# Batch 7's attention moves out of the plain blocks into the first contraction of the second layer's second pair

## The chip, the core and the metric

One core of a Trainium2 chip runs the whole program. The metric is the device time of one execution in microseconds (us). The engines are named as in the profile: PE (TensorE matmul) with its weight loads PEld, DVE (VectorE), ACT (ScalarE), POOL (GpSimd) and SP (SyncE, which issues most DMAs). Each engine takes its instructions in the order in which the program holds them; SP and ACT also issue DMAs from that order.

## What is computed

```python
kv  = einsum('bhsd,bhse->bhde', k, v)          # 8 batches, 8 heads, s = 576, d = 64
out = einsum('bhsd,bhde->bhse', q, kv)
x   = out / sqrt(mean(out*out, -1) + 1e-6) * g_norm     # -> 4608 tokens x 512
h   = x @ w_in1                                # 512 -> 2048
g   = where(h >= 1, h, where(h <= -1, 0, (h + 1)**2 / 4))
x1  = g @ w_out1                               # 2048 -> 512
r   = maximum(x1 @ w_in2, 0)
out = (r * r) @ w_out2
```

All of it is float32; a product of the two layers is made of three matmuls on values split into a high and a low part (`hi*hi + hi*lo + lo*hi`).

## The kernel before

**Two stretches.** Batches 0 to 4 go through layer 1 as plain blocks of 512 tokens (`h_stage`, `out_stage`, matmuls of line 246). Everything else is done in pairs of token blocks by a seven-product scheme (fewer multiplications, more additions): `PAIRS = [(1, 5), (2, 0), (2, 2), (1, 7), (2, 4), (2, 6)]`, each a layer and its first block, and a short rest step at the end. Steps are counted n = 0 to 6; n = 2 is layer 2's second pair.

**A step of a pair** has a first contraction (`in_phase(n)`, 512 to 2048) and a second one (`out_phase(n)`, 2048 to 512), 336 matmuls each, all of line 927. The first goes through four quarters q = 0 to 3; a quarter has seven products p in the order `PRODUCTS = (1, 6, 2, 7, 5, 4, 3)`, and each product has two halves k = 2q and 2q + 1 of six matmuls. Products 1 and 2 of a half add up in one PSUM bank (named `ph2_1_k`), 6, 7 and 4 in a second (`ph2_6_k`), 5 and 3 in a third (`ph2_5_k`); so `ph2_5_3<-x2_2_3_0` is product 3 of half 3. In between the bank is read: DVE adds (`e16`, `e167` at line 977, `h` at line 984), ACT applies the ReLU and the square in place (lines 991, 992). At the end of a quarter DVE makes sums of the results (`t1`, `g2`, lines 1000 and 1001). The second contraction takes operands t that ACT rounds to the high part (line 225) and DVE completes with the low part (line 856), three ahead (`LEAD = 3`); its first eight (`t2_1_0` to `t2_1_7`) stand in a ring of five slots, three of pool `gp` and two of `wp`.

**Attention** of one batch is four head pairs hp. `kv_stage` makes k-transposed times v of two head pairs in one PSUM bank (`pkv`), ACT copies it to `kvbd`; `t_stage` transposes q on DVE (`qT`, line 564); `o_stage` makes each half of the output (`po`, line 591), which ACT reads three times (squares `s2` and `wk0`, scaled `wk1`; lines 596, 597, 217) and DVE once (`s2lo`, line 602); `r_stage` sums squares on PE (`pr`, line 616), then ACT takes Ln, Exp and a square (lines 617, 619, 232) and DVE a Newton step and the scaling (lines 530, 533, 534). `po`, `pr` and `pkv` share the two banks of pool `ps_t` (tag `at`). The tiles `wk0`, `wk1`, `wk2`, `hl0` and `hl1` have one buffer each; `wk2` holds `s2` first and then `t`.

**Where attention stands.** In the plain stretch hooks put it between the plain blocks, at numbered half steps: `STARTS` gives the first of each head pair of batches 2 to 7. Batch 7 has no plain block; its results `xt`, `xr` go to DRAM (`keep_x`, lines 640 and 641) and are read back as input of step 3 (`x2_jobs`). Its four head pairs are spread over batches 4 to 6 and one behind them.

**What sets the order.** The tile layer records the program and then a list scheduler writes each engine's order by its own estimate of readiness, so an instruction can stand far from its place in the source. A tile waits for the last user of its buffer.

Of the kernel before, what the change touches and what calls it, by code (L numbers as in the profile page):

```python
# [76 lines left out]
def linear_attention_rms_two_mlps(  # L77
# [12 lines left out]
    nc = tc.nc  # L90
# [18 lines left out]
    STARTS = (32, 39, 46, 53, 60, 66, 72, 78, 84, 90, 96, 102, 109, 115, 121, 127, 133, 139)  # L109
    STARTS += (145, 151, 156, 161, 166, 173)  # L110
# [30 lines left out]
    PAIRS = [(1, PLAIN), (2, 0), (2, 2), (1, B - 1), (2, 4), (2, 6)]  # L141
    LAST_B = B - 1
# [461 lines left out]
    def r_stage(b, hp):  # L604
# [63 lines left out]
    def attention(starts, order):  # L668

        slots = []  # L670
        for j, (s, (b, hp)) in enumerate(zip(starts, order)):
            turn.setdefault((b, hp), len(turn))
            if b == 1:
                slots += [(max(0, s - 7), load_kv, b, hp), (s, kv_stage, (b, hp))]
            elif j % 2 == 0:
                two = order[j : j + 2]
                turn[two[1]] = len(turn)
                slots += [(max(0, s - 7), load_kv, *i) for i in two]
                slots.append((s, kv_stage, *two))
            slots += [  # L680
                (max(0, s - 7), load_q, b, hp),
                (s, t_stage, b, hp),
                (s + 3, o_stage, b, hp, 0),
                (s + 4, o_stage, b, hp, 1),
            ]
            if hp == 0 and b < LAST_B:
                slots.append((s + 6, begin, b))
            slots.append((s + 6, r_stage, b, hp))
            if b == LAST_B:
                slots.append((s + 8, keep_x, b, hp))  # L690
            elif hp == NP - 1:
                slots.append((max(2 * NF * b, 0) if b < PLAIN + 1 else s + 9, store_xrem, b))
        return slots
# [129 lines left out]
    t1_ring = Ring(*[(st, "st")] * 7, (dt, "dt3"))  # L823
    v_ring = Ring(*((wp, f"w0_{i}") for i in (12, 13)))
# [35 lines left out]
    def width(n):  # L860
        return TB if n < NS else H2
# [73 lines left out]

    FIRST = (1, 6, 5)
# [4 lines left out]
    def in_phase(n):  # L941
# [3 lines left out]
        def tile(ring, name):  # L945
            return ring.tile([P, TB], F32, name)[:, :N]

        for q in range(NQ):
            ps = {}
            e = {}  # L950
            for p in PRODUCTS:
                w = take_w2(layer(n), 0, q, p)
                for i in range(2):
# [11 lines left out]
                    if p == 1:  # L965
                        e[i, 1] = tile(e_ring, f"e1_{n}_{k}")
# [157 lines left out]
    def outputs(n, hn, hm):  # L1124
# [7 lines left out]
        t = (t_ring if n < NS - 1 else v_ring).tile([P, 2, TB], F32, f"ov{n}_{hn}_{hm}")  # L1132
# [26 lines left out]
    order = []  # L1159
    for b in range(2, LAST_B):  # L1160
        order += [(LAST_B, b - 4)] * (b >= 4) + [(b, hp) for hp in range(NP)]
    order.append((LAST_B, NP - 1))
    jobs += attention(STARTS, order)
# [202 lines left out]
```

## Time and profile before

| | |
|---|---|
| median of 3 runs | 1554.6 us (1552.7 to 1554.84) |
| the profiled execution's own time | 1553.93 us |
| its span, first to last instruction | 1552.2 us |
| PE busy | 1541.5 us (99%) |
| DVE / ACT busy | 1140.9 us (74%) / 971.2 us (63%) |
| granted TensorE clock | 1.00 |

The span is what the trace covers; the own time holds 1.7 us beside it. Busy is the union of an engine's instructions; matmuls are pipelined, so their records overlap.

### The profile page before, as it was taken

How to read it: one execution, taken by the hardware profiler on the slowest of the kernel's cores; microseconds unless marked ns; L12 is line 12 of the kernel's file. 1: busy time of each engine (PE TensorE's matmuls, PEld its weight loads, DVE VectorE, ACT ScalarE, POOL GpSimd, SP SyncE). 2: the span in 40 equal slices, each digit the busy share in tenths (PEclk: the TensorE clock that was granted, in tenths of full speed). 3: DMA queues.
4: the chain of work that ended last, by engine and by line, in shares of the span. 5: the costliest groups of instructions: out<-in, count | busy, mean ns of one | idle time of the engine just before them, and what ended most of it. 6: DMA issues, size and time to landing. Idle time of an engine off the chain costs nothing.

```text
span 1552.2 us, 22204 instructions
## 1 busy us (share of the span) xinstructions
PE 1541.5 (99%) x7631; PEld 1274.0 (82%) x7633; DVE 1140.9 (74%) x1991; ACT 971.2 (63%) x1833; POOL 14.0 (1%) x38
## 2 busy tenths in 40 slices
PE   9999999999999999999999999999999999999999
PEld 5787888888788888888888888888888888888899
DVE  6986787777777866974597559778965596558666
ACT  5977677667667677654575466456646663666374
POOL 0000000000000000000000000000000000000000
PEclk9999999999999999999999999999999999999999
DMA  9666998998896944686576877687876676977796
GB/s 288 191 224 174 279 310 253 295 309 256 252 278 214 286 147 160 196 261 208 165 251 194 221 218 251 193 229 210 259 224 205 205 240 196 242 250 203 233 391 251
DMA packets 322431, 365.07 MB, mean 235 GB/s; under 512 B 197008, under 2 KB 222608, under 8 KB 322320
## 3 DMA queue, kind: packets, MB, share of 16 engines
q1 hardware_dynamic: 293472, 311.75, 67.6%
q10 hardware_dynamic: 28848, 51.91, 9.0%
q8 instruction: 61, 1.00, 0.3%
q14 instruction: 50, 0.41, 0.1%
HBM read 283.64 MB, written 79.95 MB: 234 GB/s over the span
## 4 chain that ended last, share of the span: by engine, by line
PE 96%; ACT 1%; DVE 1%; DMA 1%; issue 0%; ACTq 0%; DVEq 0%
PE po L927 32%; PE ph L927 27%; PE ph L246 18%; PE acc L246 14%; PE po L591 1%; PE pkv L487 1%; PE pr L616 1%; DMA x1d<-ev 1%; PE pwarm L1221 1%; DMA wt<-wsd 0%; ACT raw L276 0%; ACT w L225 0%; DVE t L530 0%; PE pr L545 0%; ACT u L726 0%
## 5 line engine op out<-in xcount | busy, mean ns | idle before, releaser
L927 PE MATMUL po<-t,ws 128*128 128x512 f32 x2016 | 457.9, 389 | 0.0
L927 PEld LDWEIGHTS po<-t,ws 128*128 128x128 f32 x2016 | 378.5, 188 | 78.5
L927 PE MATMUL ph<-x,ws 128*128 128x512 f32 (+1 forms) x2016 | 422.1, 371 | 0.0
L927 PEld LDWEIGHTS ph<-x,ws 128*128 128x128 f32 x2016 | 355.9, 188 | 65.5
L246 PE MATMUL ph<-x,w 128*128 128x512 f32 x1344 | 335.1, 397 | 1.4 <-ACT w L225 0.6
L246 PEld LDWEIGHTS ph<-x,w 128*128 128x128 f32 x1344 | 249.6, 188 | 57.6 <-ACT w L225 1.4
L856 DVE TENSOR_TENSOR t<-g,t 128x512 fp32r<-128x512 f32 (+1 forms) x336 | 216.8, 651 | 92.9 <-ACT t L225 91.1
L225 ACT CAST t<-g 128x512 fp32r<-128x512 f32 (+1 forms) x336 | 196.6, 590 | 122.4 <-DVE t L856 63.6
L984 DVE TENSOR_TENSOR h<-ph,e 128x512 f32<-128x512 f32 (+1 forms) x144 | 93.1, 646 | 68.2 <-PE ph L927 60.4
L246 PE MATMUL acc<-gs,w 128*128 128x512 f32 x528 | 133.6, 397 | 2.1 <-DVE u L728 1.6
L246 PEld LDWEIGHTS acc<-gs,w 128*128 128x128 f32 x528 | 98.1, 188 | 23.6 <-DVE u L728 2.0
L991 ACT ACTIVATE h<-h 128x512 f32<-128x512 f32 (+1 forms) x120 | 70.3, 585 | 60.1 <-DVE h L984 55.3
L246 PE MATMUL acc<-gs,wt 128*128 128x512 f32 x432 | 107.9, 397 | 0.0
L977 DVE TENSOR_TENSOR e<-ph,e 128x512 f32<-128x512 f32 (+1 forms) x96 | 61.0, 644 | 51.6 <-PE ph L927 50.8
L246 PEld LDWEIGHTS acc<-gs,wt 128*128 128x128 f32 x432 | 80.5, 188 | 17.4
L726 ACT ACTIVATE u<-ph,halfb 128x512 f32<-128x512 f32 x80 | 55.2, 690 | 53.4 <-PE ph L246 53.1
L728 DVE SCALAR_TENSOR_TENSOR u<-u,ph 128x512 f32<-128x512 f32 x80 | 54.6, 683 | 33.7 <-ACT u L232 33.5
L992 ACT ACTIVATE g<-h 128x512 f32<-128x512 f32 (+1 forms) x120 | 70.7, 589 | 3.2
L225 ACT CAST gs<-u 128x512 fp32r<-128x512 f32 x80 | 49.9, 623 | 36.1 <-DVE u L728 29.4
L225 ACT CAST x<-xr 128x512 fp32r<-128x512 f32 (+1 forms) x84 | 48.9, 585 | 37.5 <-DVE xr L907 19.6
L238 DVE TENSOR_TENSOR gs<-u,gs 128x512 fp32r<-128x512 f32 x80 | 54.8, 685 | 18.6 <-ACT gs L225 18.2
L991 ACT ACTIVATE u<-ph 128x512 f32<-128x512 f32 (+1 forms) x40 | 22.1, 553 | 62.6 <-PE ph L927 61.8
(144 smaller groups left out, 1597.6 us busy)
## 6 DMA issues: line engine op xcount, KB each, us to landing
ws<-wsd SPq DMA_DIRECT2D x364, 512.0 KB, 4.4
wsd<-s ACTq DMA_DIRECT2D x80, 512.0 KB, 4.3
wt<-wsd SPq DMA_DIRECT2D x36, 512.0 KB, 5.3
raw<-in_moe_w_in_dram SPq DMA_DIRECT2D x32, 512.0 KB, 5.5
raw<-in_moe_w_out_dram SPq DMA_DIRECT2D x32, 512.0 KB, 6.4
xr<-x1d SPq DMA_DIRECT2D x36, 256.0 KB, 4.8
out_dram<-ov SPq DMA_DIRECT2D x142, 64.0 KB, 4.0
wsd<-w SPq DMA_DIRECT2D x17, 512.0 KB, 4.5
```

The source lines that it names most:

```text
L225: return e.copy(dst, src)
L238: lo = engine(op + "_lo", phase).tensor_tensor(t[:, 1, :], src, t[:, 0, :].bitcast(F32), ALU.subtract)
L246: nc.tensor.matmul(dst, wt(a), xt(c), start=first and n == 0, stop=last and n == 2)
L487: nc.tensor.matmul(ps[s, d], lhs, rhs, start=c == 0, stop=c == MR)
L726: nc.scalar.activation(u, ps, AF.Relu, bias=halfb, scale=0.5)
L728: nc.vector.scalar_tensor_tensor(u, u, 1.0, ps, op0=ALU.min, op1=ALU.max)
L856: engine2(op + "_lo").tensor_tensor(t[:, 1, :], src, t[:, 0, :].bitcast(F32), ALU.subtract)
L927: nc.tensor.matmul(ps, wt(a), xt(c), start=first and n == 0 and i == 0, stop=last and n == len(lhs) - 1 and i == 2, skip_group_check=True,)
L977: nc.vector.tensor_tensor(e[i, p], bank, e[i, 1], ALU.add)
L984: nc.vector.tensor_tensor(h, bank, add, ALU.add)
L991: nc.scalar.activation(u, h, AF.Relu)
L992: nc.scalar.activation(g, u, AF.Square)
```

## The change

Batch 7's attention leaves the plain stretch (`STARTS` now holds twenty entries for batches 2 to 6, mostly seven half steps apart) and is run by a function `host` from a table `in_host`, at steps of step 2's first contraction: `attention((0, 6, 12, 18), ...)`, one unit being one product of both halves. Loads begin at -7, inside step 1's second contraction, and the last store comes at 29, inside step 2's second one. For batch 7 `o_stage` and `r_stage` stand one step later than for the others and `keep_x` eleven steps behind the start, four behind `r_stage`. To make room, during that contraction: the two `at` banks belong to attention alone (six of eight are left to the products), the temporaries `h` and `u` have three slots in place of six, the `e` tiles of a quarter stand as pairs in the three `gp` slots (`e_pairs`), and `xt` and step 1's output tiles `ov` share the two `wp` slots (ring `idle`). Keys and values of head pairs 2 and 3 are loaded into the `dt` slots. Step 1's outputs are stored at products 0, 1, 3, 4 in place of 0, 1, 5, 9.

```diff
+    HOST = 2
...
+            if b == LAST_B and hp > 1:
+                pool, tag = dt, f"dt{2 * hp + n - 4}"
...
-        xt = st.tile([P, TB], F32, tag="st", name=f"xt_{hp}")
         nc.vector.scalar_tensor_tensor(t, t, -3.0, y, op0=ALU.add, op1=ALU.mult)
-        nc.vector.tensor_tensor(xt, o[:, :TB], t[:, :TB], ALU.mult)
-        xr = ap1.tile([P, REM], F32, tag="xr", name=f"xr_{hp}")
-        nc.vector.tensor_tensor(xr, o[:, TB:], t[:, TB:], ALU.mult)
-        x_kept[hp] = xt, xr
+        xt = idle.tile([P, 2, TB], F32, f"xt_{hp}").rearrange("p a s -> p (a s)")
+        nc.vector.tensor_tensor(xt[:, :S], o, t, ALU.mult)
+        x_kept[hp] = xt
...
-                (s + 3, o_stage, b, hp, 0),
-                (s + 4, o_stage, b, hp, 1),
+                (s + 3 + (b == LAST_B), o_stage, b, hp, 0),
+                (s + 4 + (b == LAST_B), o_stage, b, hp, 1),
...
-            slots.append((s + 6, r_stage, b, hp))
+            slots.append((s + 6 + (b == LAST_B), r_stage, b, hp))
             if b == LAST_B:
-                slots.append((s + 8, keep_x, b, hp))
+                slots.append((s + 11, keep_x, b, hp))
...
+    idle = Ring(*((wp, f"w0_{i}") for i in (NF - 2, NF - 1)))
+    e_pairs = Ring(*[(gp, "g")] * 3)
+    banks_at = [(ps_t, "at")] * 2
...
+    def keep_e(n, e, i, p, k):
+
+        if n != HOST:
+            e[i, p] = e_ring.tile([P, TB], F32, f"e{p}_{n}_{k}")[:, : width(n)]
+        elif i == 0:
+            t = e_pairs.tile([P, 2, TB], F32, f"e{p}_{n}_{k}")
+            e[0, p], e[1, p] = t[:, 0], t[:, 1]
...
+    jobs += attention(STARTS, [(b, hp) for b in range(2, LAST_B) for hp in range(NP)])
+    in_host = {}
+    for at, *job in attention((0, 6, 12, 18), [(LAST_B, hp) for hp in range(NP)]):
+        in_host.setdefault(at, []).append(job)
...
+    def host(i):
+        for at in sorted(a for a in in_host if a <= i):
+            for f, *a in in_host.pop(at):
+                f(*a)
...
+        if n == HOST:
+            ps_ring.slots = [a for a in ps_ring.slots if a not in banks_at]
+            tmp.slots = [(ep, "e")] * 3
         for i, _ in enumerate(step_in):
+            if n == HOST:
+                host(i)
...
+                if n == HOST - 1 and i % 2 == 0:
+                    host(i // 2 - 7 * NQ)
+                elif n == HOST and i % 2 == 0:
+                    host(i // 2 + 7 * NQ)
```

**The first place: PE, the seam between quarters 1 and 2 of step 2's first contraction.** Before, PE goes from product 4 through product 3 of halves 2 and 3 straight into quarter 2, whose first row is `ph2_1_4`:

```order
L927 MATMUL ph2_6_3_8751<-x2_2_4_1_8358,ws2_0_1_4_8631 128x512 x3
L927 MATMUL ph2_5_2_8811<-x2_2_3_0_8132,ws2_0_1_3_8655 128x512 x3
L927 MATMUL ph2_5_2_8811<-x2_2_3_1_8335,ws2_0_1_3_8655 128x512 x3
L927 MATMUL ph2_5_3_8822<-x2_2_3_0_8132,ws2_0_1_3_8655 128x512 x3
L927 MATMUL ph2_5_3_8822<-x2_2_3_1_8335,ws2_0_1_3_8655 128x512 x3
L927 MATMUL ph2_1_4_8885<-x2_2_1_0_8003,ws2_0_2_1_8688 128x512 x3
```

Now, behind product 4, the first eight matmuls of `pkv_7_2`, the first half of `pr_7_1` and two matmuls of product 3 (not shown):

```order
L490 MATMUL pkv_7_2_8728<-rest0_127 64x64 x2
L931 MATMUL ph2_5_2_8670<-x2_2_3_0_7890,ws2_0_1_3_8489 128x512
L931 MATMUL ph2_5_2_8670<-x2_2_3_1_8093,ws2_0_1_3_8489 128x512 x3
L931 MATMUL ph2_5_3_8681<-x2_2_3_0_7890,ws2_0_1_3_8489 128x512 x3
L490 MATMUL pkv_7_2_8728<-v_7_3_8527,k_7_3_8524 64x64 x8
L490 MATMUL pkv_7_2_8728<-rest1_128 64x64 x2
L931 MATMUL ph2_5_3_8681<-x2_2_3_1_8093,ws2_0_1_3_8489 128x512 x3
L619 MATMUL pr_7_1_1_8783<-s2_7_1_8662,ones_121 128x288
L619 MATMUL pr_7_1_1_8783<-s2lo_7_1_8699,ones_121 128x288
L594 MATMUL po_7_2_0_8864<-qT_7_2_8755,kvbd0_129 128x288
L931 MATMUL ph2_1_4_8803<-x2_2_1_0_7761,ws2_0_2_1_8535 128x512 x3
```

Two products' seam now holds the end of head pair 1's `pr` and the first `po` of head pair 2, and both stand ahead of all of quarter 2.

**The second place: DVE at the same seam.** Before, behind the last `h` of quarter 1 stand its sums and then the first `e16` of quarter 2:

```order
L984 TENSOR_TENSOR h2_3_3_8873<-ph2_5_3_8822,e16_2_3_8758 128x512
L1000 TENSOR_TENSOR t1_2_2_8877<-g2_2_2_0_8726 128x512
L1001 TENSOR_TENSOR g2_2_2_0_8726<-g2_2_2_1_8727,g2_2_2_0_8726 128x512
L1038 TENSOR_TENSOR g2_2_2_0_8726<-g2_2_2_1_8727,t1_2_2_8877 128x512
L1000 TENSOR_TENSOR t1_2_3_8880<-g2_2_3_0_8737 128x512
```

Now the Newton step of head pair 1 (`t_7_1<-pr_7_1`) stands among the sums, and the transpose `qT_7_2` behind all of it:

```order
L533 SCALAR_TENSOR_TENSOR t_7_1_8788<-pr_7_1_0_8779,t_7_1_8788 128x288
L533 SCALAR_TENSOR_TENSOR t_7_1_8788<-pr_7_1_1_8783,t_7_1_8788 128x288
L1008 TENSOR_TENSOR t1_2_3_8798<-g2_2_3_0_8587 128x512
L632 SCALAR_TENSOR_TENSOR t_7_1_8788<-t_7_1_8788,wk0_7_1_8557 128x576
L1009 TENSOR_TENSOR g2_2_3_0_8587<-g2_2_3_1_8588,g2_2_3_0_8587 128x512
L634 TENSOR_TENSOR xt_1_8793<-wk1_7_1_8558,t_7_1_8788 128x576
L567 STREAM_TRANSPOSE qT_7_2_8755<-q_7_2_8530 128x576
L985 TENSOR_TENSOR e6_2_4_8833<-ph2_6_4_8826,e1_2_4_8810 128x512
```

So seven rows stand between the end of `pr_7_1` and the operand of `po_7_2_0`.

**The third place: DVE where the first contraction ends and the second begins.** Before, the low parts of `t2_1_0` to `t2_1_4` stand earlier, among the rows of quarters 0 to 2, and behind the last `h` come the sums and then the sixth:

```order
L984 TENSOR_TENSOR h2_3_7_9185<-ph2_5_7_9134,e16_2_7_9081 128x512
L1000 TENSOR_TENSOR t1_2_6_9189<-g2_2_6_0_9049 128x512
L1001 TENSOR_TENSOR g2_2_6_0_9049<-g2_2_6_1_9050,g2_2_6_0_9049 128x512
L856 TENSOR_TENSOR t2_1_5_9237<-g2_2_5_0_8904,t2_1_5_9237 128x512
L1000 TENSOR_TENSOR t1_2_7_9192<-g2_2_7_0_9060 128x512
```

Now all eight stand behind the last `h`, the first of them behind `xt_3`:

```order
L632 SCALAR_TENSOR_TENSOR t_7_3_9116<-t_7_3_9116,wk0_7_3_8919 128x576
L992 TENSOR_TENSOR h2_3_7_9163<-ph2_5_7_9096,e6_2_6_9021 128x512
L634 TENSOR_TENSOR xt_3_9121<-wk1_7_3_8920,t_7_3_9116 128x576
L860 TENSOR_TENSOR t2_1_0_9173<-g2_2_0_0_8346,t2_1_0_9173 128x512
L1008 TENSOR_TENSOR t1_2_6_9167<-g2_2_6_0_8999 128x512
L860 TENSOR_TENSOR t2_1_1_9176<-g2_2_1_0_8356,t2_1_1_9176 128x512
L1009 TENSOR_TENSOR g2_2_6_0_8999<-g2_2_6_1_9000,g2_2_6_0_8999 128x512
L1008 TENSOR_TENSOR t1_2_7_9170<-g2_2_7_0_9009 128x512
L860 TENSOR_TENSOR t2_1_2_9179<-g2_2_2_0_8577,t2_1_2_9179 128x512
L1009 TENSOR_TENSOR g2_2_7_0_9009<-g2_2_7_1_9010,g2_2_7_0_9009 128x512
L1046 TENSOR_TENSOR g2_2_0_0_8346<-g2_2_0_1_8347,t1_2_0_8561 128x512
L860 TENSOR_TENSOR t2_1_3_9193<-g2_2_3_0_8587,t2_1_3_9193 128x512
```

Their slots are the reason: `t2_1_0`, `t2_1_1` and `t2_1_4` take the three `gp` slots, which hold quarter 3's `e` pairs until its last reads, and `t2_1_2` and `t2_1_3` take the two `wp` slots, which hold `xt_2` and `xt_3` until their stores have landed.

## Rows read from the trace of the kernel before

**Rows 1.** The page's head: the span, and busy time of each engine.
```profile
span 1552.2 us, 22204 instructions
...
PE 1541.5 (99%) x7631; PEld 1274.0 (82%) x7633; DVE 1140.9 (74%) x1991; ACT 971.2 (63%) x1833; POOL 14.0 (1%) x38
```
**Rows 2.** Busy time by stretch: step 1's second contraction, step 2's first, step 2's second.
```profile
core 0: us, PE busy (x) PEld busy (x) DVE busy (x) ACT busy (x) POOL busy (x), PEclk, DMA share, GB/s
782.10:858.20 76.10, 76.10 (x337) 63.06 (x336) 65.19 (x106) 43.36 (x75) 0.00 (x0) 1.00 0.72 220
858.20:934.40 76.20, 76.20 (x337) 63.10 (x337) 43.64 (x66) 44.22 (x74) 0.00 (x0) 1.00 0.79 221
934.40:1010.50 76.10, 76.10 (x337) 63.05 (x336) 63.80 (x103) 42.20 (x73) 0.00 (x0) 1.00 0.72 222
```
**Rows 3.** PE's waits: who for whom, us in total, times, longest.
```profile
PE po L591 <- DVE t L530: 1.1, 1, 1.1
...
PE acc L246 <- ACT ev L781: 0.5, 1, 0.5
```
**Rows 4.** Instructions by line and shape: count, busy us, mean ns of one, idle before.
```profile
L225 ACT CAST t<-g 128x512 fp32r<-128x512 f32 x288 | 177.1, 621 | 111.4 <-DVE t L856 63.3 <-PE po L927 46.0 <-DVE x L856 0.7
...
L984 DVE TENSOR_TENSOR h<-ph,e 128x512 f32<-128x512 f32 x120 | 82.9, 691 | 62.2 <-PE ph L927 54.8 <-ACT h L991 7.1
...
L991 ACT ACTIVATE h<-h 128x512 f32<-128x512 f32 x96 | 60.6, 631 | 54.6 <-DVE h L984 49.8
...
L217 ACT ACTIVATE wk<-po,gvec 128x288 f32<-128x288 f32 x56 | 28.7, 513 | 0.0
...
L617 ACT ACTIVATE wk<-pr,lnb 128x288 f32<-128x288 f32 x56 | 27.0, 501 | 5.9 <-PE pr L616 5.8
L530 DVE SCALAR_TENSOR_TENSOR t<-pr,t 128x288 f32<-128x288 f32 x64 | 26.4, 452 | 10.2 <-ACT t L232 7.9 <-issue 2.2
...
L619 ACT ACTIVATE wk<-wk,expb 128x576 f32<-128x576 f32 x28 | 22.0, 787 | 0.2
...
L596 ACT ACTIVATE s<-po 128x288 fp32r<-128x288 f32 x52 | 21.3, 411 | 6.2 <-PE po L591 3.1 <-DVE x L238 1.7 <-PE po L246 1.1
...
L564 DVE STREAM_TRANSPOSE qT<-q 128x576 f32<-128x576 f32 x26 | 20.1, 775 | 9.7 <-PE po L591 9.6
...
L602 DVE TENSOR_TENSOR s2lo<-wk,s 128x576 fp32r<-128x576 f32 x26 | 19.6, 752 | 3.0 <-ACT wk L597 2.9
...
L232 ACT ACTIVATE t<-wk 128x576 f32<-128x576 f32 x28 | 19.2, 687 | 0.3
...
L533 DVE SCALAR_TENSOR_TENSOR t<-t,wk 128x576 f32<-128x576 f32 x24 | 18.1, 754 | 0.3
...
L225 ACT COPY kvbd<-pkv 64x64 f32<-64x64 f32 x48 | 9.9, 207 | 20.0 <-PE pkv L487 19.4
```
**Rows 5.** DVE in order of time where step 2's second contraction begins: start, us.
```profile
934.91 0.69 DVE L984 TENSOR_TENSOR h<-ph,e 128x512 f32<-128x512 f32 x1 [0.67 <-ACT h L991]
935.60 0.69 DVE L1000 TENSOR_TENSOR t<-g 128x512 f32<-128x512 f32 x1
936.33 0.69 DVE L1001 TENSOR_TENSOR g<-g,g 128x512 f32<-128x512 f32 x1
936.94 0.69 DVE L856 TENSOR_TENSOR t<-g,t 128x512 fp32r<-128x512 f32 x1
```
**Rows 6.** DMA issues by line: count, KB each, median us from issue to landing.
```profile
xpd<-xt SPq DMA_DIRECT2D x4, 256.0 KB, 5.3
```
**Rows 7.** The matmuls that open the program: ns min/median/max, first and last start.
```profile
L1221 PE MATMUL pwarm<-warm x11: 609/634/634, 1.2 to 5.4; 128*128 128x512 bf16 x11
```
**Rows 8.** First-layer matmuls of the plain stretch, columns as in rows 4.
```profile
L246 PE MATMUL ph<-x,w 128*128 128x512 f32 x1344 | 335.1, 397 | 1.4 <-ACT w L225 0.6 <-DVE kv L227 0.4 <-DVE t L530 0.3
```

More of the change, by code (lines that the diff above doesn't have):

```diff
@@ L108, in linear_attention_rms_two_mlps @@
     WHOLE = ((1, 0), (1, 1))
[L109 to L110 removed]
+    STARTS = (32, 39, 46, 53, 61, 68, 75, 82, 92, 99, 106, 113, 122, 129, 136, 143)
+    STARTS += (151, 156, 161, 166)
     SECOND = (37, 46, 55.2, 64.6, 73.2, 85, 93.6, 102.2, 110.8, 120.4, 128.8, 137.4, 146)
@@ L677, in attention @@
                 turn[two[1]] = len(turn)
-                slots += [(max(0, s - 7), load_kv, *i) for i in two]
+                slots += [(s - 7, load_kv, *i) for i in two]
                 slots.append((s, kv_stage, *two))
             slots += [
-                (max(0, s - 7), load_q, b, hp),
+                (max(0, s - 7) if b < LAST_B else s - 7, load_q, b, hp),
                 (s, t_stage, b, hp),
-                (s + 3, o_stage, b, hp, 0),
-                (s + 4, o_stage, b, hp, 1),
+                (s + 3 + (b == LAST_B), o_stage, b, hp, 0),
+                (s + 4 + (b == LAST_B), o_stage, b, hp, 1),
             ]
@@ L687, in attention @@
                 slots.append((s + 6, begin, b))
-            slots.append((s + 6, r_stage, b, hp))
+            slots.append((s + 6 + (b == LAST_B), r_stage, b, hp))
             if b == LAST_B:
-                slots.append((s + 8, keep_x, b, hp))
-            elif hp == NP - 1:
+                slots.append((s + 11, keep_x, b, hp))
+            if b < LAST_B and hp == NP - 1:
                 slots.append((max(2 * NF * b, 0) if b < PLAIN + 1 else s + 9, store_xrem, b))
@@ L965, in in_phase @@
                     if p == 1:
-                        e[i, 1] = tile(e_ring, f"e1_{n}_{k}")
+                        keep_e(n, e, i, 1, k)
                         g2[k] = [
@@ L1131, in outputs @@
         stores = []
-        t = (t_ring if n < NS - 1 else v_ring).tile([P, 2, TB], F32, f"ov{n}_{hn}_{hm}")
+        ring = idle if n == HOST - 1 else t_ring if n < NS - 1 else v_ring
+        t = ring.tile([P, 2, TB], F32, f"ov{n}_{hn}_{hm}")
         for m in range(2):
@@ L1158, in linear_attention_rms_two_mlps @@
     jobs += attention((0, 7, 14, 21), [(1, hp) for hp in range(NP)])
[L1159 to L1163, printed above, removed]
+    jobs += attention(STARTS, [(b, hp) for b in range(2, LAST_B) for hp in range(NP)])
+    in_host = {}
+    for at, *job in attention((0, 6, 12, 18), [(LAST_B, hp) for hp in range(NP)]):
+        in_host.setdefault(at, []).append(job)
     for job in sorted(jobs, key=lambda j: j[0]):
@@ L1286, in linear_attention_rms_two_mlps @@
     rows_left = []
+    def host(i):
+        for at in sorted(a for a in in_host if a <= i):
+            for f, *a in in_host.pop(at):
+                f(*a)
     for n in range(NS + 1):
         step_in = in_phase(n) if n else ()
+        if n == HOST:
+            ps_ring.slots = [a for a in ps_ring.slots if a not in banks_at]
+            tmp.slots = [(ep, "e")] * 3
         for i, _ in enumerate(step_in):
+            if n == HOST:
+                host(i)
             pay(True)
-            if late and i in (0, 1, 5, 9) and n < NS:
+            if late and i in ((0, 1, 5, 9) if n != HOST else (0, 1, 3, 4)) and n < NS:
                 late.pop(0)()
@@ L1304, in linear_attention_rms_two_mlps @@
             break
+        if n == HOST:
+            ps_ring.add(*banks_at)
+            tmp.slots = [a for i in range(3) for a in ((ep, "e"), (dt, f"dt{i}"))]
         result[n] = result_of(dict(g2))
@@ L1307, in linear_attention_rms_two_mlps @@
         if n < NS - 1:
-            for _ in steps:
+            for i, _ in enumerate(steps):
                 pay(True)
+                if n == HOST - 1 and i % 2 == 0:
+                    host(i // 2 - 7 * NQ)
+                elif n == HOST and i % 2 == 0:
+                    host(i // 2 + 7 * NQ)
             if n == 0:
```

12 lines of the change are left out of this document (4 added, 8 removed).

## Prediction

> **What bounds the kernel now.** I read the page's head first, then the busy times by stretch, then who makes PE wait. PE is busy 1541.5 of 1552.2 us [rows 1]: the reader is to see that no other engine comes near, so the time is what PE has to do plus what it waits. In a pair's step this is exact: a contraction of 336 matmuls takes 76.1 us and PE is busy for all of them, 0.2265 us a matmul, the granted clock 1.00 [rows 2]. A half product (six matmuls) is 1.36 us, a product 2.72. DVE works 43.6 and ACT 44.2 us of the 76.2 in the contraction that is to be host, so by the sums there is room. PE's waits behind the start-up are few: 1.1 us where a `po` waits for DVE's Newton step, 0.5 where an accumulation waits for an eviction on ACT [rows 3]. That first one matters twice: it is a gain if it goes, and it shows what a `po` costs whose bank or operand hangs on work queued in DVE.
>
> **What the change removes.** PE's instructions are the same ones at another place: moved, not saved, 0. DVE loses four small multiplies of batch 7, 0 on PE. What can be saved is waits in the plain stretch: at most 1.1 + 0.5 = 1.6 us [rows 3], at least 0. The Newton wait belongs to head pairs six half steps apart, now mostly seven; I take it as gone and the other as staying: **-1.1**.
>
> **What it adds by busy time.** Per head pair DVE gets a transpose 0.775, `s2lo` 0.752, two Newton steps 0.90, two of 0.75: 3.9 us, four times 15.7. ACT gets 8 x (0.41 + 0.41 + 0.51) = 10.6, 4 x (1.00 + 0.79 + 0.69) = 9.9, sixteen copies of 0.207 = 3.3: 23.9 us [rows 4]. DVE comes to 59 us, ACT to 68 [rows 2] in a stretch that attention's own matmuls lengthen beyond 76. By sums it is hidden under PE; if queues ran in the best order the term would be 0. They run in the order written, and at two places of that order PE stands still.
>
> **The first place: the seam of quarters 1 and 2.** I count from PE's end of product 5 of quarter 1, with durations of [rows 4] and PE's pace of [rows 2].
> DVE takes that product's `h` (0.69) and then `xt_0` (0.75): 1.44. Only then is `wk2` free for head pair 1's `s2`, which ACT has queued behind the ReLU and square of that same `h`: these end at 0.69 + 0.63 + 0.63 = 1.95. ACT's three reads of each half of `po_7_1` then end at 3.28 and 4.61, the last-but-one at 4.10, and `s2lo` on DVE at 4.85.
> PE has done product 4 at 2.72, but `pkv_7_2` needs the bank that ACT leaves at 3.28; with 0.4 us of it (a guess, and the same work with or without waits) PE is at 3.7, and `pr_7_1` needs `s2lo`: done at 5.1. Product 3 and the pieces of `pkv` between (2.72 + about 0.65): 8.5.
> DVE's two `h` of product 4 stand behind `s2lo`: 5.54 and 6.23. ACT works on them and on `pr_7_1`: ReLU 6.17, square 6.80, ReLU 7.43, Ln 7.93, square 8.56, ReLU 9.19, then four copies out of `pkv_7_2`: 10.0. They free the bank for the second half of `pr_7_1`, which PE ends at 10.3.
> Now PE's next row is `po_7_2_0`, which reads `qT_7_2`. ACT: square 10.65, Ln 11.15, Exp 11.94, ReLU 12.57, square 13.26. DVE: Newton twice 14.16, a sum 0.69, scaling 0.75, a sum 0.69, `xt_1` 0.75 = 17.05, and the transpose 17.8. All of quarter 2 is queued behind that `po`.
> Without waits PE would be there at 2.72 + 0.4 + 0.27 + 2.72 + 0.65 + 0.27 = 7.0. The place costs 17.8 - 7.0 = **+10.8**. Below: if everything up to the end of `pr_7_1` were covered and only what must lie between it and the `po` counted, 0.50 + 0.79 + 0.69 + 0.90 + 0.75 + 0.75 + 0.78 = 5.2. Above: `xt_0` and `xt_1` also wait until step 1's outputs have left the slots, behind which SP's loads for head pairs 2 and 3 and quarter 2's weights are queued; if one more landing of 5.3 us [rows 6] shows there, 16.1. I take 10.8, because no row says that those landings are late.
>
> **The second place: the end of the first contraction.** Zero is now PE's last matmul of it. `pr_7_3` ends 5.44 us (two products) earlier. Behind it on ACT: Ln, ReLU, Ln, square, Exp, ReLU, square = 4.37, at -1.07. DVE: Newton twice -0.17, `h` 0.52, scaling 1.27, the last `h` 1.96, `xt_3` 2.71, and only then the low part of `t2_1_0`, 3.4, which PE wants at 0.45 (after the high part of both halves): 2.9 late. Before, DVE did the sixth t there, at 936.94 [rows 5], the five ahead of it being ready. It does not stay at 2.9: `t2_1_3` needs the slot of `xt_3`, whose store leaves at 2.71 and lands 5.3 later [rows 6], 8.0; ACT's cast 0.62, DVE's low part 0.69, PE's remaining four matmuls 0.91: 10.2, due at 4 x 1.36 = 5.4 (the store of the 64 left tokens is issued behind it, so a little more): **+5.0**. Below 2.9, if the store were early; above 7, since for each of the first eight t DVE has two operations of 0.69 against PE's 1.36 and cannot catch up.
>
> **The clock.** Since start-up PE never idles over 1.1 us at a time [rows 3] and the granted clock reads 1.00 [rows 2]. The matmuls that opened the program, out of idleness, started 0.42 us apart (eleven from 1.2 to 5.4 us) [rows 7], not 0.2265. A wait of 7.5 us (10.3 to 17.8) is far from 1.1; if it ends like the start, eleven matmuls lose 0.19 us each, 2.1. Bounds 0 and 2.1; I take **+2.1**. [...] No trace here shows a fall in the middle of a run.
>
> **Sum**, against the profiled execution's own 1553.9 (the median of the runs shown is 0.7 above it): 1553.9 - 1.1 + 10.8 + 5.0 + 2.1 = 1570.7, rounded **1571**.
>
> **The rivals.**
> Both places wait but the clock stays: 1568.6.
> Only one of the places bites: the first with the clock 1565.7, the second alone 1557.8. For it: each hangs on the order of one queue. Against: both waits are on instructions that stand in that order.
> It is longer: DMAs land late at the seam (16.1 for 10.8), or other quarters wait too, with six banks and three temporaries: 1576 and up.
> Everything is hidden, since by busy time it fits: 1552.8, no change. It would need PE to reach `po_7_2_0` 5.2 us or more after `pr_7_1` with nothing in between.
> Faster: the plain stretch's matmuls take 335.1 / 1344 = 0.249 us [rows 8], 0.023 above a pair's. I put that down to attention's own matmuls overlapping them in the records. If it were pressure by attention's ACT and DVE work, 1344 x 0.023 = 31 us over batches 1 to 7, batch 7's seventh of 4.4 us would go: 1553.9 - 1.1 - 4.4 = 1548.4, if the host waited nowhere. It decides as long as the two places together stay under 5.5 us, against 15.8 by my count.
>
> **How the numbers follow.** Forecast 0.50, clock holds 0.13, one place only 0.17 (0.10 and 0.07), longer 0.09, hidden 0.07, faster 0.04. The range takes the lower bounds, 1553.9 - 1.6 + 5.2 + 2.9 = 1560.4, and above 1553.9 + 16.1 + 7 + 2.1 = 1579.1: 1560 to 1579, which leaves out the second place alone, the hidden and the faster cases and the tail, 2 in 10. A measurement of this kernel tells some 0.2% (3.1 us) from no change. Slower by more: 0.89, the first four cases; within: 0.08, the hidden case and a little of the faster one; faster 0.03.
>
> **What would show it.** Right: in the host contraction a PE wait of some 7 us for DVE's transpose (`po<-qT`), shorter ones for ACT before it, and at the head of the second contraction waits for ACT's and DVE's t; that contraction near 81 us where it was 76.1, the host stretch some 13 us longer than its matmuls; the clock below 1.00 in the wait's window. Wrong: a PE without waits in the host, or the same waits with another releaser, above all a DMA of weights. I would be wrong at the root if DVE reached `qT_7_2` before PE ended `pr_7_1`.

## The result, and the profile after

The changed kernel takes 1565.6 us (median of 6 runs, 1564.55 to 1565.99) where the one before takes 1554.1 (6 runs beside it): a ratio of 1.0074, 95% interval 1.0061 to 1.0087. It is slower, by 11.5 us. 1571 was forecast, 17 us slower; the sign, the place and the kind of the loss are as forecast, the size was not. The profiled execution's own time is 1565.67.

The page's head, as in [rows 1]:

```profile
span 1563.9 us, 22197 instructions
...
PE 1544.8 (99%) x7631; PEld 1274.1 (81%) x7633; DVE 1141.2 (73%) x1987; ACT 971.2 (62%) x1833; POOL 14.8 (1%) x38
```

The first and the second place are counted as in the forecast: the seam of quarters 1 and 2, where PE and DVE meet, and the end of the first contraction, which stands third in the section on the change.

PE still reads 99%, with 3.3 us more busy time than in [rows 1] for the same 7631 matmuls. The span grew by 11.7, so some 8.4 us are idle time that PE did not have before. PE's waits tell whom it waited for (lines of this kernel: 594 is the `po` of attention, 567 the transpose `qT`, 931 the pairs' matmuls, 860 and 226 a `t`'s low part and cast, 218 the scaled copy out of `po`):

```profile
PE po L594 <- DVE qT L567: 6.6, 1, 6.6
PE po L931 <- DVE t L860: 1.7, 1, 1.7
...
PE po L931 <- ACT t L226: 0.6, 1, 0.6
...
PE pkv L490 <- ACT wk L218: 0.4, 1, 0.4
...
PE pr L619 <- ACT wk L218: 0.3, 1, 0.3
```

All five are new, all five lie in step 2, and the two waits of [rows 3] are gone. (A sixth new one, 0.5 us for DVE at 15.4 us, lies in the start-up and is in no experiment. The wait for the eviction on ACT is back in all experiments but one, with 0.2 to 1.6 us in their profiled executions; it stands at some 440 us, in the plain stretch, far ahead of what their edits move.) Busy time by stretch, columns as in [rows 2]: step 2's first contraction, its second one, then the long wait and the time behind it.

```profile
846.20:942.70 96.50, 89.05 (x450) 71.78 (x449) 50.64 (x81) 57.64 (x117) 0.00 (x0) 0.96 0.73 199
942.70:1022.40 79.70, 77.44 (x338) 62.87 (x338) 70.68 (x115) 45.31 (x78) 0.00 (x0) 1.00 0.71 215
892.80:899.50 6.70, 0.12 (x1) 0.00 (x0) 5.65 (x10) 3.07 (x6) 0.00 (x0) 0.75 1.02 368
899.50:903.00 3.50, 3.45 (x8) 2.69 (x9) 0.00 (x0) 1.10 (x3) 0.00 (x0) 0.50 0.96 244
```

The host contraction takes 96.5 us and the one behind it 79.7; both took 76.1 or 76.2 [rows 2]. Every later full contraction is at 76.1 to 76.3 again. While PE waits, DVE is busy for 5.65 of 6.7 us and ACT for less than half: a chain that goes from ACT to DVE. Behind the wait the granted clock is 0.50 for 3.5 us: the pairs' matmuls there start 0.43 us apart (901.10, 901.52, 901.95) and not 0.2265, so some eight matmuls take the time of sixteen: 1.75 us lost.

The plain stretch ends 12.3 us earlier (the second contraction of step 0 begins at 617.7 and began at 630.0). So the balance of the spans is -12.3 + (96.5 - 76.1) + (79.7 - 76.1) = 11.7.

The chain at the first place, in order of time. PE, from the end of head pair 1's `pr` to the first `po` of head pair 2:

```profile
892.62 0.29 PE L619 MATMUL pr<-s2lo,ones 128*128 128x288 f32 x1
899.55 0.85 PE L594 MATMUL po<-qT,kvbd 128*128 128x288 f32 x1 [6.63 <-DVE qT L567]
```

ACT, on that `pr`: Ln, Exp and the square that DVE's Newton step needs:

```profile
893.01 0.50 ACT L620 ACTIVATE wk<-pr,lnb 128x288 f32<-128x288 f32 x1
893.55 0.78 ACT L622 ACTIVATE wk<-wk,expb 128x576 f32<-128x576 f32 x1
...
894.75 0.67 ACT L233 ACTIVATE t<-wk 128x576 f32<-128x576 f32 x1
```

DVE: the last `h` of product 5 (the zero of the forecast's count), then, twelve us on, the Newton step and everything that stands between it and the transpose:

```profile
883.29 0.69 DVE L992 TENSOR_TENSOR h<-ph,e 128x512 f32<-128x512 f32 x1 [0.72 <-ACT h L999]
...
895.45 0.82 DVE L533 SCALAR_TENSOR_TENSOR t<-pr,t 128x288 f32<-128x288 f32 x2 [1.01 <-ACT t L233]
896.18 0.68 DVE L1008 TENSOR_TENSOR t<-g 128x512 f32<-128x512 f32 x1
896.78 0.75 DVE L632 SCALAR_TENSOR_TENSOR t<-t,wk 128x576 f32<-128x576 f32 x1
897.45 0.68 DVE L1009 TENSOR_TENSOR g<-g,g 128x512 f32<-128x512 f32 x1
898.05 0.75 DVE L634 TENSOR_TENSOR xt<-wk,t 128x576 f32<-128x576 f32 x1
898.72 0.77 DVE L567 STREAM_TRANSPOSE qT<-q 128x576 f32<-128x576 f32 x1
```

The last seven operations, from 895.45 to 899.49, leave no gap. The transpose needs nothing of the rows above it; it only stands behind them in DVE's order. The `po` takes the bank of the first half of `pr`, which the first Newton operation leaves at 895.9; the other 3.6 us of its wait are for `qT` alone. And PE's whole next quarter stands behind that `po`.

The second place, DVE from the last result of the attention on:

```profile
943.70 0.75 DVE L634 TENSOR_TENSOR xt<-wk,t 128x576 f32<-128x576 f32 x1
944.36 0.68 DVE L860 TENSOR_TENSOR t<-g,t 128x512 fp32r<-128x512 f32 x1
...
949.85 0.69 DVE L860 TENSOR_TENSOR t<-g,t 128x512 fp32r<-128x512 f32 x1 [0.59 <-ACT t L226]
```

and ACT's cast of the fourth `t`, which waits for the store of `xt` to have left its buffer:

```profile
949.20 0.62 ACT L226 CAST t<-g 128x512 fp32r<-128x512 f32 x1 [0.86 <-DMA xpd<-xt]
```

PE's matmuls of the second contraction begin at 942.67; the low part of the first `t` ends at 945.0. Both halves of the forecast's second place are here: a first `t` behind `xt_3`, and a fourth that waits for the store of a result. The two waits come to 2.3 us; the rest of the 3.6 are starts of matmuls next to them that come 0.1 to 0.2 us late each.

### The profile page after: what moved, and what is told of

It is laid out like the page before. It is cut to its first block, busy times and chain, and to the rows that moved or that the text cites. A ratio compares the mean times of both kernels' runs of the same rounds, so it can differ in the third digit from the quotient of the medians.

```text
span 1563.9 us, 22197 instructions
## 1 busy us (share of the span) xinstructions
PE 1544.8 (99%) x7631; PEld 1274.1 (81%) x7633; DVE 1141.2 (73%) x1987; ACT 971.2 (62%) x1833; POOL 14.8 (1%) x38
## 4 chain that ended last, share of the span: by engine, by line
PE 95%; ACT 2%; DMA 2%; DVE 1%; issue 0%; SPq 0%; DVEq 0%; ACTq 0%
PE po L931 32%; PE ph L931 27%; PE ph L247 19%; PE acc L247 14%; PE po L594 2%; PE pkv L490 1%; PE pr L619 1%; DMA ws<-wsd 0%; DMA raw<-in_moe_w_in_dram 0%; DMA q<-in_q_dram 0%; ACT raw L277 0%; ACT w L226 0%; DMA xr<-xrd 0%; DMA xr<-xpd 0%; DVE t L533 0%
## 5 line engine op out<-in xcount | busy, mean ns | idle before, releaser
L931 PE MATMUL ph<-x,ws 128*128 128x512 f32 (+1 forms) x2016 | 427.9, 373 | 0.0
L247 PE MATMUL ph<-x,w 128*128 128x512 f32 x1344 | 329.9, 395 | 1.3 <-ACT w L226 0.6
L239 DVE TENSOR_TENSOR gs<-u,gs 128x512 fp32r<-128x512 f32 x80 | 54.9, 686 | 18.4 <-ACT gs L226 17.8
```

What stands on the lines that cost most here:

```text
L239: lo = engine(op + "_lo", phase).tensor_tensor(t[:, 1, :], src, t[:, 0, :].bitcast(F32), ALU.subtract)
L247: nc.tensor.matmul(dst, wt(a), xt(c), start=first and n == 0, stop=last and n == 2)
L931: nc.tensor.matmul(ps, wt(a), xt(c), start=first and n == 0 and i == 0, stop=last and n == len(lhs) - 1 and i == 2, skip_group_check=True,)
```

## The experiments

Two questions: which order makes PE wait (PE's own, DVE's, SP's), and what the halved clock costs. All kernels are the changed one with the edit shown. A ratio is to the kernel before on the same chip; the changed kernel's is 1.0074 (1.0061 to 1.0087).

### Load one q four steps earlier

```diff
-                (max(0, s - 7) if b < LAST_B else s - 7, load_q, b, hp),
+                (max(0, s - 7) if b < LAST_B else s - 7 - 4 * (hp == 2), load_q, b, hp),
```

> One number is changed: q of batch 7's head pair 2 is loaded four steps earlier, ahead of step 1's last output stores on SP. The transpose qT of that pair then stands on DVE in the middle of quarter 1 and no longer behind the Newton step of pair 1, and on PE the po that reads it stands behind product 2 of quarter 2, no longer at the seam. Theory of the order (PE waits because this po is queued in front of a ready quarter while DVE's order serves it last): the wait of 6.6 us for qT goes, the granted clock stays at 1.00 and so the 3.5 us at half clock (1.75 us lost) go too: 1565.6 - 6.6 - 1.8 = 1557 us. Rival, transfers (loads of pair 2 and weights of quarter 2 stand late on SP and PE would stand there anyway): the wait turns into one for ws, k or v, and the time stays above 1562. Rival, throughput of DVE and ACT: the waits come back elsewhere in quarters 2 and 3 and the time falls by less than 4 us, above 1561.5.

Measured: 1559.2 us, ratio 1.0040 (1.0027 to 1.0052). DVE now makes the transpose in quarter 1, and PE reaches the `po` behind three more products without waiting:

```profile
877.97 0.78 DVE L567 STREAM_TRANSPOSE qT<-q 128x576 f32<-128x576 f32 x1 [1.96 <-PE po L594]
```
```profile
893.80 8.47 PE L931 MATMUL ph<-x,ws 128*128 128x512 f32 x36
902.11 0.65 PE L594 MATMUL po<-qT,kvbd 128*128 128x288 f32 x2
```

Its two contractions of step 2:

```profile
846.40:935.30 88.90, 87.69 (x449) 70.64 (x448) 50.49 (x81) 57.38 (x117) 0.00 (x0) 1.00 0.78 215
935.30:1015.70 80.40, 78.70 (x338) 64.11 (x338) 70.75 (x115) 45.14 (x78) 0.00 (x0) 0.98 0.71 214
```

The host contraction falls by 7.6 us and its clock stays at 1.00. The theory of the order stands; it had promised 8.4, of which 0.35 came back as a wait for weights. The second contraction did not get shorter but longer by 0.7: its wait of 1.7 us is unchanged, and in the profiled execution the clock fell behind it (the trace has it at half from 938.2 to 941.6).

### Move only PE's row

```diff
+        if (b, hp, half) == (LAST_B, 2, 0):
+            late = last_e[1, 4][:, 0, :P]
+            nc.tensor.matmul(ps[:, :P], kvbd[turn[b, hp] % 2], late, start=True, stop=True)
...
+            last_e[p, k] = t
```

> Only PE's order at the first place is changed: ahead of the first po of head pair 2 stands a matmul of 128 columns without use (into the po's own bank, overwritten by it) that reads the first sum of quarter 2, so the po can't be queued before that quarter's first product; on PE it now stands behind product 2 of quarter 2. DVE's order is as in the changed kernel up to there: qT still stands behind Newton, scaling and xt_1, and q is loaded as late. Theory (the wait is one of PE's order: a ready quarter is queued behind one late po): PE runs three products, 8.2 us, while DVE gets to qT, and the wait of 6.6 us and the half clock go as with q loaded early: 1565.6 - 8.4 = 1557.2, at most 2 us more if weights land late. Rival (DVE's lateness itself costs: what stands behind qT on DVE is late for quarter 2 as well): waits of PE for DVE's sums follow in quarter 2, and the time stays above 1560.

Measured: 1558.7 us, ratio 1.0026 (1.0016 to 1.0036). DVE ends `qT` as late as ever, at 899.9, and nobody minds (line 935 is the pairs' matmul here, 597 the `po`):

```profile
893.45 8.46 PE L935 MATMUL ph<-x,ws 128*128 128x512 f32 x36 [0.15 <-DMA ws<-wsd]
901.75 0.38 PE L595 MATMUL po<-e,kvbd 128*128 128x128 f32 x2
901.97 0.65 PE L597 MATMUL po<-qT,kvbd 128*128 128x288 f32 x2
```

Its two contractions:

```profile
846.50:935.20 88.70, 87.72 (x453) 70.83 (x451) 50.49 (x81) 57.33 (x117) 0.00 (x0) 1.00 0.79 222
935.20:1016.00 80.80, 78.73 (x337) 64.09 (x337) 70.76 (x115) 45.67 (x78) 0.00 (x0) 0.98 0.70 206
```

The host contraction is 88.7 us, as with q loaded early. So a late `qT` by itself costs nothing. What costs is that PE's order has the `po` in front of 8.5 us of ready matmuls. (The run before had moved both orders, since with the transpose early PE's row moved too; DVE's order alone was not tried. By the rows above the `po` would then still have waited for its bank.) Most of the distance to 1557.2 is again the second place: the wait of 1.7 us with the clock at 0.98 over the contraction, which takes 80.8.

### Fill PE's wait

```diff
+        if (b, hp, half) == (LAST_B, 2, 0):
+            given.append(ps_ring.tile([P, TB], F32, "fill"))
+            for _ in range(10):
+                x = x2[HOST, 1, 0][:, 0, :].bitcast(F32)
+                nc.tensor.matmul(given[0], kvbd[turn[b, hp] % len(kvbd)], x, start=True, stop=True)
...
-                (s + 3 + (b == LAST_B), o_stage, b, hp, 0),
+                (s + 3 + (b == LAST_B) - 3 * ((b, hp) == (LAST_B, 2)), o_stage, b, hp, 0),
...
+                        ps[i, bank_of[p]] = given.pop() if given else tile(ps_ring, f"ph{n}_{p}_{k}")
```

> Ten float32 matmuls of 128x512 without use are put on PE straight ahead of the po that waits 6.6 us for qT, into the bank that product 1 of quarter 2 overwrites next; the orders of PE, DVE, ACT and SP are otherwise those of the changed kernel. By the po of the plain stretch (0.27 us for 288 columns) they take some 4.9 us, inside the wait. Nothing that the po waits for is moved. Theory of the clock (it falls because PE stands idle, and what it costs is 3.5 us at half speed): the granted clock stays at 1.00 in the quarter that follows, the wait shrinks to 1.7 us, and the time falls by 1.7 us to 1563.9. Rival (the clock falls for another reason, or its fall costs nothing since PE waits again later): the clock falls in the same stretch, or the time stays within 0.5 us of 1565.6. If the matmuls take more than 6.6 us, the time rises by what they take beyond that.

Measured: 1566.0 us, ratio 1.0081 (1.0068 to 1.0095): no change, but not for the rival's reason. The matmuls took 8.6 us and not 4.9 (twenty records from 893.5 to 902.1), the `po` came 1.8 us after its operand, and the clock stayed at 1.00. (The 4.9 rested on a misreading of the plain stretch's `po`, which is told at the end.) 1565.6 + 1.8 - 1.75 = 1565.7 would be the sum; a test in which two effects cancel shows neither. So it was run again with columns cut from 512 to 384.

```diff
-                nc.tensor.matmul(given[0], kvbd[turn[b, hp] % len(kvbd)], x, start=True, stop=True)
+                nc.tensor.matmul(given[0][:, :384], kvbd[turn[b, hp] % len(kvbd)], x[:, :384], start=True, stop=True)
```

> The ten matmuls of the run before filled more than the wait: each has two records of 0.43 us, 8.6 us in all, so the po came 1.9 us later than its operand, and the time did not move although the clock stayed at 1.00. Now they have 384 columns and not 512: 10 x 2 x 0.32 = 6.5 us, which ends about when qT is ready. (Both halves of the po now stand at the seam together; DVE and SP have a few rows in another order behind it.) Theory of the clock (an idle PE loses its clock, and that costs 3.5 us at half speed): the granted clock stays at 1.00 and the time is 1.8 us below the changed kernel's, 1563.8. Rival (the fall costs nothing that the wait doesn't hide): 1565.6, no change.

Measured: 1563.6 us (1562.89 to 1565.07), ratio 1.0060 (1.0048 to 1.0072).

```profile
894.35 6.61 PE L596 MATMUL fill<-x,kvbd 128*128 128x384 f32 x20
901.15 1.24 PE L599 MATMUL po<-qT,kvbd 128*128 128x288 f32 x4 [0.18 <-DVE qT L567]
```

```profile
847.80:942.60 94.80, 93.80 (x470) 74.29 (x469) 50.65 (x81) 57.63 (x117) 0.00 (x0) 1.00 0.75 202
```

The `po` is as late as before, with work that nobody needs in the gap, and the kernel is 2.0 us faster, where 1.8 was expected. The intervals of the two ratios overlap (1.0061 to 1.0072 lies in both), so the medians alone do not settle it. The contraction of 94.8 for 96.5 and the clock of 1.00 for 0.96 agree with it, and so does the mean granted clock of whole executions, 0.999 or 1.000 in all five where the changed kernel's six have 0.997 or 0.998. (The profiled execution is the longest of the five: the wait for the eviction takes 1.6 us of it.) By these rows PE paid for the wait of 6.63 us and then again, 1.75, for the clock.

### The second place: other buffers, earlier stores, an earlier end

First the buffers (the ring of the `t` tiles begins with the buffer of `xt_2`) together with earlier stores, then the earlier stores alone:

```diff
-                slots.append((s + 11, keep_x, b, hp))
+                slots.append((s + 8, keep_x, b, hp))
...
+            t_ring.slots = [(wp, f"w0_{NF - 2}")] + [(gp, "g")] * 3 + [(wp, f"w0_{NF - 1}")]
```

> Only the second place is changed: the ring of the t tiles starts the second contraction of step 2 with the buffer that held xt_2, then the three that hold quarter 3's sums, and the buffer of xt_3 last; and the results are stored eight steps behind the start and not eleven. The low part of the first t then stands on DVE ahead of the last six h. Theory (the first t are late because their buffers are): the wait of 1.7 us for t on DVE goes, and the one of 0.6 us for ACT's cast too or nearly; with the refilling of PE behind each the second contraction falls from 79.4 to about 76.5 us: 1565.6 - 3 = 1562.6. Rival (DVE has too much to do at the seam, whatever the buffers: it needs two operations for every t and is behind from the last h on): the wait moves to the second or third t and the contraction stays above 78.5 us, the time above 1564.5. The wait of 6.6 us at the first place and the halved clock behind it stay in either case.

> One part of the change alone is undone: the results of batch 7 are stored eight steps behind the start and not eleven. Theory of the order: the first place is as it was (6.6 us for qT, the clock at half for 3.5 us); at the second place the store of xt_2 leaves earlier and frees its buffer, so one of the five first t is prepared ahead of the last h, but the first t still waits for the buffers of quarter 3's sums: within 1.5 us of 1565.6. Rival (the late stores are what makes the second contraction late): the second contraction falls from 79.4 to about 76.5 us, the time to 1562.7.

Measured: 1567.3 us, ratio 1.0091 (1.0076 to 1.0106), and 1565.9, ratio 1.0074 (1.0062 to 1.0086). Neither gains. With the buffers changed the wait of 1.7 us is broken up and not removed:

```profile
PE po L931 <- ACT t L226: 1.0, 2, 0.6
...
PE po L931 <- DVE t L860: 0.5, 1, 0.5
```

and the contraction takes 78.9 us. This theory (the first `t` are late because their buffers are) fell for the most part; its rival, that the wait only moves, had 78.5 or more. (The profiled execution, 1565.4 us, is the fastest of the four; what makes the others 2 us longer is in no trace.) With the stores alone it takes 79.5. When the results are stored is not what the change costs.

Then both places together (the edit of q and the two above), and both with the last head pair one step earlier, so that its Newton step, scaling and `xt_3` stand among the `h` of products 5 and 4:

> Both places are mended together: q of head pair 2 is loaded four steps earlier, and the ring of the t tiles begins with the buffer of xt_2, with the results stored eight steps behind the start. Theory of the order: the gains add. With q alone the kernel took 1559.2, with a second contraction of 80.2 us in which a wait of 1.7 us brought the clock to half for 3.3 us; the slots alone broke that wait into three of at most 0.6 us, a contraction of 78.8. Together: 1559.2 - 80.2 + 78.8 = 1557.8, the clock at 1.00 throughout. Rival (the clock falls behind shorter waits as well): 1559 or more.

```diff
-    for at, *job in attention((0, 6, 12, 18), [(LAST_B, hp) for hp in range(NP)]):
+    for at, *job in attention((0, 6, 12, 17), [(LAST_B, hp) for hp in range(NP)]):
```

> As the run with both places mended, and the last head pair starts at step 17 and not 18, so that its Newton step, its scaling and its result stand on DVE among the h of products 5 and 4 of the last quarter and no longer behind the last h. Theory (the second place is late because the end of the attention and the first t want DVE at the same time): the first t come in time, the second contraction falls to 76.5 us or less, and the time to 1557.8 - 2.3 = 1555.5; it is not below 1553.7, since the waits of 0.4, 0.3 and 0.4 us at the first place stay and nothing is saved anywhere else but the 1.6 us of the plain stretch. Rival (the two operations of DVE for each t are themselves the limit): above 1557.

Measured: 1559.5 us, ratio 1.0033 (1.0020 to 1.0045), and 1556.0, ratio 1.0010 (1.0001 to 1.0018). The gains did not add in the first of the two: at the first place the clock was at half from 890.7 to 894.1, behind three waits of PE of 0.4, 0.3 and 0.9 us within 3 us (ACT twice, then weights; in the next run, with much the same waits spread over 8 us, it stayed at 1.00), and at the second place, where the wait for DVE is 1.6 us again and stands behind one of 0.7 for ACT, it fell once more (0.98 over the contraction): 80.8 us, none of the gain. The rival, "1559 or more", was right. In the second run next to nothing is left of the second place:

```profile
847.10:936.80 89.70, 87.87 (x451) 70.96 (x450) 54.27 (x86) 59.90 (x120) 0.00 (x0) 1.00 0.78 217
936.80:1013.40 76.60, 76.60 (x338) 62.97 (x337) 67.23 (x110) 42.97 (x76) 0.00 (x0) 1.00 0.73 221
```

So the second place is a collision in time: the end of the attention and the first `t` want DVE together. With the end of the attention out of its way DVE keeps up, and PE shows no wait there. At 1556.0 this is the best of the hosted versions and still a little behind the kernel before. Waits of 1.8 us are left in its host contraction; without them it would take 1554.2, and the kernel before takes 1554.6, so nothing here points to a version that beats it by more than can be measured.

### Without the attention

Batch 7's attention is left out (its loads stay, and parts of k are stored in place of its results); then the same with step 1's output stores at the times of the other steps.

```diff
...
-                f(*a)
+                if f in (load_kv, load_q):
+                    f(*a)
+                elif f is o_stage and a[-1] == 0:
+                    keep_x(*a[:2])
```

> Batch 7's attention is left out: its loads stay, and parts of its k are stored in place of its results, so step 3 works on other values (the output is not the reference's). It gives the price of that attention at either place. Theory: the plain stretch gains nothing but the attention's own matmuls and the 1.6 us of waits, and the host loses by waiting. The plain stretch is 12.3 us shorter after the change, so this kernel should come to 1553.9 - 12.3 = 1541.6 (own time), both contractions of step 2 at 76.1 us and no wait of PE over 0.5 us behind the start-up: attention costs 12.3 us in the plain stretch and 24 in the host. Rival (the host stretch is long for its other new arrangements, three temporaries, six banks, sums in other buffers, and not for attention's order): the contractions stay above 78 us each and the time above 1545.

```diff
-            if late and i in ((0, 1, 5, 9) if n != HOST else (0, 1, 3, 4)) and n < NS:
+            if late and i in (0, 1, 5, 9) and n < NS:
```

> As the run without batch 7's attention (again the output is not the reference's), and step 1's output stores leave at the times of the other steps, after products 0, 1, 5 and 9 of step 2 and not 0, 1, 3 and 4, so that eight stores no longer stand on SP ahead of the weights of product 3 of quarter 1. That run took 1548.4 with a wait of PE of 3.6 us for these weights and the clock at half for some 5.8 us behind it, where 1541.6 had been expected. Theory (the weights are late because SP issues the stores, which wait for DVE's transposes, ahead of them): the wait goes, the clock stays at 1.00, and the time falls by 3.6 + 2.9 to 1541.9. Rival (the DMA queues are simply full in this stretch): the wait stays or turns up at the next weights, and the time is above 1546.

Measured: 1548.4 us, ratio 0.9968 (0.9956 to 0.9979), and 1541.4, ratio 0.9915 (0.9901 to 0.9928). The first missed the theory, and the rival is half right: an arrangement of the change is at fault, but none that it named, and only the first of the two contractions is long (82.8 us, the second 76.2). Its long wait is for weights, and SP shows why (start, us until the last of the group, issues):

```profile
PE ph L933 <- DMA ws<-wsd: 3.6, 1, 3.6
```

```profile
875.77 5.66 SPq L1132 DMA_DIRECT2D out_dram<-ov  x8
881.54 0.46 SPq L849 DMA_DIRECT2D ws<-wsd  x1
```

```profile
882.40:886.10 3.70, 0.07 (x2) 0.05 (x1) 1.88 (x3) 2.32 (x5) 0.00 (x0) 0.86 0.94 222
886.10:891.90 5.80, 5.80 (x14) 4.30 (x15) 1.71 (x3) 1.85 (x4) 0.00 (x0) 0.50 1.02 283
```

Eight output stores, moved forward by the change, stand on SP ahead of the weights of product 3 of quarter 1. With the stores later again, both contractions take 76.1 us, no such wait is left, and 1541.4 is what the shorter plain stretch had promised (1541.6):

```profile
846.50:922.60 76.10, 76.10 (x337) 63.03 (x336) 42.60 (x65) 42.99 (x72) 0.00 (x0) 1.00 0.91 253
922.70:998.80 76.10, 76.10 (x337) 63.04 (x336) 65.68 (x107) 43.98 (x75) 0.00 (x0) 1.00 0.73 218
```

In the changed kernel these weights stand on SP behind as many stores; the attention's own matmuls and waits cover it, and it shows in two versions with q loaded early: 0.4 us, and 0.9 with the two edits of the second place besides. (The 0.8 us of the version with the last head pair earlier are for the first weights of quarter 2, another row.)

This run gives the price of batch 7's attention: 1554.6 - 1541.4 = 13.2 us in the plain stretch (medians on one chip; the traces have 12.3), and 11.5 more, 24.7, in the host.

## Why the prediction was right in kind and 5 us too long

**What bounds.** Right. PE's matmuls were moved and not saved. In the host the attention takes 96.5 - 76.1 - 7.45 (its four waits of 0.44, 0.30, 0.07 and 6.63) - 1.75 (clock) = 11.2 us of PE, and the plain stretch lost 12.3. The difference is the **-1.1** of the forecast in size, in part by luck: both waits of [rows 3] went, 1.6 us, where the forecast let one of them stay, and the 0.5 us between is not traced. The rival "faster" (pressure of attention's ACT and DVE work on the plain matmuls) is refuted: a seventh of 31 us was not there to be had.

**The first place.** The mechanism held row by row: `wk2` behind `xt_0`, the second half of `pr_7_1` behind ACT's four copies, then the wait for `qT`. The term, **+10.8**, was mis-sized; measured are 7.45 us of waits. Two steps failed. "Without waits PE would be there at 7.0": PE came at 16.2 (899.5, counted from 883.3), and 16.2 - 7.45 = 8.8; the small matmuls of `pkv` and `pr` and the changes between them and the pairs' take 1.8 more than the guess. And 17.8 for the end of `qT` is 16.2, because rows were added up at the full length of their records. On DVE they start 0.60 to 0.67 apart where they last 0.68 to 0.75, but that is only 0.5 of the 1.6: from the Newton step on it takes 4.0 us and not 4.5. The other 1.1 lie ahead of that step, which begins at 12.2 and not at 13.3, and most of them on ACT, whose reads of a `po` start 0.29 apart where they last 0.4 to 0.5:

```profile
885.22 0.39 ACT L599 ACTIVATE s<-po 128x288 fp32r<-128x288 f32 x1
885.51 0.40 ACT L600 ACTIVATE wk<-po 128x288 f32<-128x288 f32 x1
885.80 0.50 ACT L218 ACTIVATE wk<-po,gvec 128x288 f32<-128x288 f32 x1
```

PE's wait for the transpose itself, some 7 us forecast, is 6.63.

**The second place.** Forecast **+5.0**, measured 79.7 - 76.1 = 3.6, again with the right rows. "2.9 late" for the first `t` is 1.7: its low part ends 2.4 us after the second contraction begins and not 3.4. The fourth `t` waits for the store, as written, but its cast begins 6.5 us in and not 8.0, and PE, which had waited already, waits 0.56 more for it.

**The clock.** Forecast **+2.1** from the start of the program, measured 1.75 (3.5 us at half). The short fill shows that it is a cost of its own (1563.6 us for 1565.6). That the clock would fall in the middle of a run was the author's estimate, from the opening matmuls [rows 7], and the changed kernel shows such a fall: the granted clock is 0.50 behind the wait of 6.63 us, and stays at 1.00 when work without use fills that wait. One reading ahead of it was too narrow: "never idles over 1.1 us" leaves out a wait of 1.55 us for DVE at 54.5 us, behind which the clock stayed at 1.00.

Sum by measured terms: 1553.9 - 1.1 + 7.45 + 3.6 + 1.75 = 1565.6; measured 1565.67. The forecast's terms are 5.1 too long together: 3.35 at the first place, 1.4 at the second, 0.35 for the clock.

**The rivals.** "One place only" and "hidden" are refuted by the waits above. That "the first with the clock", 1565.7, is the measured time is chance: it leaves out the second place's 3.6 us, and has 3.7 too much for the first place and its clock. "Longer" falls as well: no wait of PE in the host contraction is for a DMA. "It would need PE to reach `po_7_2_0` later" was close to a recipe: put behind product 2 of quarter 2, the `po` waits for nothing.

**What the prediction left open.** It named both orders, PE's and DVE's, and could not say which to blame. DVE's rows ahead of the transpose are only the length of the wait; that there is one is PE's order, and one row moved there cures it with DVE as late as before.

## What to carry to other kernels

When independent work is hosted in a stretch that PE fills, ask of every one of its rows on the busy engine what stands behind it: here a late operand cost 6.63 us with the `po` that reads it ahead of 8.5 us of ready matmuls, and nothing with the `po` behind them. Moving matmuls between two stretches that PE fills already bought no more than the waits that the old place had, here 1.1 us net, and the new place's seams have to be free for it. A wait that is removed can uncover the next one (here 3.6 us for weights that stand behind output stores on SP), so measure the stretch without the hosted work as well.

## What the runs showed of the hardware that was not expected

Behind a wait of 1.70 us for the same `t` at the same place the clock was at half in the profiled executions of the two runs that mended only the first place (938.2 to 941.6 and 938.0 to 941.4) and not in those of the changed kernel, the two with fills and the one with earlier stores, where the contraction shows 1.00. Nor is it fixed for a kernel: the mean granted clock of an execution was 0.997 in three of the changed kernel's six and 0.998 in the others, and 0.998 to 1.000 over the eight with PE's row moved. What decides is shown by no run here.

The length of a wait was no measure here of what the clock took: behind 6.63 us PE ran 3.5 us at half, behind 3.6 us (without the attention) 5.8. In both the clock was at half for some 6.8 us, but the longer wait covered 3.3 of them and the shorter one 0.9 (the changed kernel's rows, then the other's):

```profile
892.90:896.10 3.20, 0.02 (x1) 0.00 (x0) 2.16 (x5) 2.97 (x6) 0.00 (x0) 1.00 1.04 411
896.20:899.50 3.30, 0.00 (x0) 0.00 (x0) 3.29 (x6) 0.00 (x0) 0.00 (x0) 0.50 1.00 331
882.50:885.00 2.50, 0.00 (x0) 0.00 (x0) 1.78 (x3) 1.25 (x3) 0.00 (x0) 1.00 0.88 191
885.10:886.00 0.90, 0.00 (x0) 0.00 (x0) 0.00 (x0) 0.87 (x2) 0.00 (x0) 0.50 1.15 298
```

A float32 matmul of a fill or a `po` has two records in these traces, and its price went by its columns: for 512 columns they start 0.43 us apart (0.86 in all), for 384 0.32 (0.65), for the 288 of a `po` 0.24 (0.48). The 0.27 us that the fill was first sized by is the time from a `po` to the start of the next matmul (861.33 to 861.60); that start comes 0.03 us behind the second record's, and the matmul behind it 0.45 later, at 862.05.
